# Five-group input chunks taken two at a time in front of a step, with longer rings for their results, in a Fourier-filter and MLP kernel

## The chip, the cores and the metric

The kernel runs on one core of a Trainium2 chip. Five engines work side by side, each through its own instructions in order: TensorE (PE in the profile, its weight loads PEld), VectorE (DVE), ScalarE (ACT), GpSimd (POOL) and SyncE (SP), which mostly issues DMAs. [...] The metric is the device time of one execution in microseconds, as the median of several runs. A difference of about 0.2% is what a measurement of this kernel can tell from none.

## The reference

The input `x` has 8 sequences of 3008 rows and 256 columns. A global filter in the frequency domain comes first, then an MLP with a hard swish:

```python
X = np.fft.rfft(x, axis=1)
Y = X * (filt_r + 1j * filt_i)[None, :, :]
y = np.fft.irfft(Y, n=x.shape[1], axis=1)      # (8, 3008, 256)
h = y.reshape(24064, 256) @ w_in               # 256 -> 2048
g = h * np.clip(h + 3.0, 0.0, 6.0) / 6.0
out = g @ w_out                                # 2048 -> 256
```

All of it is float32.

## The kernel before

**Two kinds of work, one stream.** The MLP is most of the work of TensorE. The 24064 rows are taken in 47 blocks of 512 rows (`NBLK`), held as 256 pairs of rows: for each pair two combined inputs, called c = 0 and c = 1. In a block, the 2048 hidden columns are taken in 8 parts of 256 (`NP`), so that there are 376 steps, counted by i = 8 k + p. A step's main loop body (the loop over `items` at the end) issues seven up products for block k, part p (`up_1` to `up_5`) and seven down products for the step before (`down`, numbered 1 to 7); it is a form of Strassen's scheme, so the up products need five sums of the inputs (tile `xt`, fields F1 to F5) beside the inputs themselves (tile `xn`).

Between the products the other engines work: up products collect in the PSUM banks `al` and `be`. ScalarE copies out of them (L990, L991 in `up_1`, L1002 in `up_2`, L1021 in `up_5`), VectorE adds (L1007, L1012), ScalarE applies the relu (L1026, twice a step), VectorE multiplies (L1031) and forms the sums of `g` that the down products need. Bank `al` is used four times a step and must have been read each time before the next product goes into it.

**The filter, spread over the steps.** The transform of the next sequences and its inverse are cut into small units. They are queued in a dictionary `plan` under a step and a place in the step's body, 0 to 4, and `do(place)` issues what stands there. Place 0 comes after `up_1`, place 1 after the first relu and ahead of `up_5`, place 2 at the end of the body. Places 3 and 4 are for units that take the banks `al` and `be`, or two banks of `psF` beside them (`a8_unit`, `b8_unit`, `bi8_unit`): place 3 comes ahead of the step, before the last step's down products, place 4 a little later, for what VectorE does with the unit's results. A step with something in place 3 has another order of its down products; in the step after it, `up_1` takes the product into `be` first and the one into `al` second.

**The last stage.** The inverse transform ends by giving the inputs of the MLP. Its work is cut into `chunks`: a sequence's 32 groups of 47 pairs each in chunks of five groups (235 pairs, "fives", `n_five`), and a rest of two or one groups (`n_unit`). `t4_load` brings a chunk's rows from DRAM with SP's queue into one of two halves of the tile `t4`. `n_five` issues 40 matmuls, each of 48 rows by 64 columns of weights and 47 columns of data (80 in the trace, as each float32 matmul is two there), into two banks of `psF`, and `ring` has ScalarE copy the results into `xn`, a ring of three blocks of pairs for each of the two halves of columns and each of c = 0 and 1 (L872; in two pieces where the ring turns round). The loop over `chunks` after `N_AT` and `FIVE_AT` decides at which step a chunk runs: in most blocks one five, in place 0 of step 1 or 6.

**The input sums.** When a chunk has completed block k, `ready` queues what forms the five sums in `xt`. Either `t_sums` does it with seven operations on GpSimd, or four copies by ScalarE (`t_copy`, L953: one of 512 columns, three of 256) and four DMAs by GpSimd's queue that add in place (`t_add`, L958, on the queue "POOLq"). With a chunk in step 1 the copies stand at the second and third step of the block and the last two adds at the sixth or seventh. `kinds` names six blocks for each sequence from the third on: "c", "a", "x" and three times "F"; `a8_unit` runs in c, a and x blocks, `b8_unit` at place 3 of step 2 and `bi8_unit` at place 3 of step 7 of each F block. All other blocks count as "t".

A remark on names: a helper records most matmuls of the last stage's rest and all MLP products under one line (L972, `strips`); the tiles tell them apart: `po<-w_all,g` are down products, `al<-xt,w_all`, `be<-xt,w_all` and those with `xn` are up products. `al<-xn,w_all` is the product of `up_5`, once a step.

## Time and profile before

| | |
|---|---|
| median of 3 runs | 2539.05 us (2538.61 to 2540.07) |
| the profiled execution | 2538.37 us, of which the span is 2536.3 us |
| granted TensorE clock | 1.000 |
| TensorE busy | 2521.5 us, 99% of the span |
| VectorE, ScalarE, GpSimd busy | 79%, 54%, 17% |
| matmuls of the fives (L899) | 3680 records, 63.6 us |
| copies into the rings (L872) | 162 from `psn`, 53.7 us |
| `t_copy` (L953) | 120, 51.9 us |

"Busy" for TensorE is a sum in which matmuls may overlap in the pipeline; where time passes is better read from the starts of successive instructions in the timeline. A line of the timeline has the start and the length in us, the engine, the line of the program, the operation, the tile written and the tiles read, the form, and how many equal instructions the line stands for; at its end, in brackets, an idle time before it and what ended that.

### The profile page before, as it was taken

To read this page: it belongs to the slowest core of one execution; us is meant where nothing else is said; L and a number is where in the kernel's file an instruction comes from. 1 tells how busy PE (TensorE), PEld (TensorE's weight loads), DVE (VectorE), ACT (ScalarE), POOL (GpSimd) and SP (SyncE) were. 2 spreads that over 40 slices of the span, in tenths; PEclk is the share of its full clock that TensorE was granted. 3 is DMA by queue.
4 is the path that set the end of the run, shared out by engine and by line. 5 is a ranking of instruction groups with operands and counts; after the bars stand their busy time and mean duration, and the time that the engine had idled before them with its cause. 6 is when DMAs were issued, how large, how long until landed. Compare 5 with 4: busy or idle time off the path is not lost.

```text
span 2536.3 us, 87284 instructions
## 1 busy us (share of the span) xinstructions
PE 2521.5 (99%) x37890; PEld 2007.7 (79%) x37890; DVE 2012.5 (79%) x3645; ACT 1363.8 (54%) x2836; POOL 423.6 (17%) x558
## 2 busy tenths in 40 slices
PE   8999999999999999999999999999999999999999
PEld 4478788888888788887888878887888878888887
DVE  6978888888787887878878788787887878767666
ACT  4554455555555555555555555555555555555554
POOL 3252111111211112111121110211102111111110
PEclk9999999999999999999999999999999999999999
DMA  8845556554445344444453443534424333211000
GB/s 237 237 121 166 162 136 157 160 135 100 119 98 137 98 103 121 97 128 101 110 125 90 125 111 95 135 88 117 122 66 96 88 103 92 54 40 27 19 22 26
DMA packets 210821, 276.91 MB, mean 109 GB/s; under 512 B 23274, under 2 KB 176392, under 8 KB 210054
## 3 DMA queue, kind: packets, MB, share of 16 engines
q1 hardware_dynamic: 163997, 200.76, 27.1%
q0 software_dynamic: 46112, 70.28, 14.2%
q8 instruction: 297, 4.87, 0.8%
q14 instruction: 86, 0.70, 0.1%
q10 hardware_dynamic: 329, 0.30, 0.0%
HBM read 164.38 MB, written 128.81 MB: 116 GB/s over the span
## 4 chain that ended last, share of the span: by engine, by line
PE 98%; DMA 1%; DVE 0%; SPq 0%; ACT 0%; issue 0%; POOL 0%; DVEq 0%
PE po L972 46%; PE al L972 26%; PE be L972 19%; PE psn L899 2%; PE be L608 1%; PE al L779 1%; PE psf L706 1%; DMA bits<-in_moe_w_in_dram 0%; PE psf L693 0%; DMA w_all<-in_x_dram 0%; PE psf L589 0%; DMA g_tmp<-t 0%; PE psn L972 0%; PE psf L763 0%; DMA wi<-wi_t 0%; DMA t<-g_tmp 0%
## 5 line engine op out<-in xcount | busy, mean ns | idle before, releaser
L972 PEld LDWEIGHTS po<-w_all,g 128*64 128x64 f32 x20808 | 1231.1, 137 | 262.5 <-issue 35.4
L972 PE MATMUL po<-w_all,g 128*64 128x128 f32 (+1 forms) x20808 | 1406.8, 274 | 0.0
L1026 ACT ACTIVATE r<-h,half_c 128x512 f32<-128x512 f32 x736 | 531.2, 722 | 335.5 <-DVE h L1007 323.4
L972 PE MATMUL al<-xt,w_all 128*64 128x256 f32 x4416 | 663.9, 379 | 0.1
L1031 DVE SCALAR_TENSOR_TENSOR g<-r,h 128x512 f32<-128x512 f32 x736 | 519.1, 705 | 147.0 <-ACT r L1026 133.5
L972 PE MATMUL be<-xt,w_all 128*64 128x256 f32 x2944 | 442.5, 379 | 0.0
L1007 DVE TENSOR_TENSOR h<-be,s 128x512 f32<-128x512 f32 x368 | 253.6, 689 | 170.3 <-PE be L972 138.5
L972 PEld LDWEIGHTS al<-xt,w_all 128*64 128x64 f32 x4416 | 285.0, 137 | 28.9 <-POOL w_all L469 1.0
L972 PEld LDWEIGHTS be<-xt,w_all 128*64 128x64 f32 x2944 | 209.0, 137 | 97.5
L1021 ACT ACTIVATE h<-al 128x256 f32<-128x256 f32 x368 | 141.4, 384 | 266.1 <-PE al L972 265.0
L1039 DVE TENSOR_TENSOR g<-g 128x512 f32<-128x512 f32 x367 | 255.7, 697 | 12.6
L1012 DVE TENSOR_TENSOR h<-al,s 128x256 f32<-128x256 f32 x368 | 155.7, 423 | 137.5 <-PE al L972 137.0
L972 PE MATMUL al<-xn,w_all 128*64 128x256 f32 (+1 forms) x1536 | 236.6, 388 | 1.0 <-DVE g L1031 0.6
L972 PE MATMUL be<-xn,w_all 128*64 128x256 f32 (+1 forms) x1536 | 236.4, 388 | 0.0
L991 ACT ACTIVATE s<-be 128x256 f32<-128x256 f32 x368 | 141.4, 384 | 148.8 <-PE be L972 145.8
L1002 ACT ACTIVATE s<-al 128x256 f32<-128x256 f32 x368 | 141.6, 385 | 123.9 <-PE al L972 120.8
L990 ACT ACTIVATE s<-al 128x256 f32<-128x256 f32 x368 | 141.7, 385 | 82.2 <-PE al L972 82.1
L1038 DVE TENSOR_TENSOR g<-g 128x256 f32<-128x256 f32 x367 | 161.9, 441 | 12.6
L1044 DVE TENSOR_TENSOR g<-g 128x256 f32<-128x256 f32 x367 | 155.5, 424 | 2.3
L972 PEld LDWEIGHTS be<-xn,w_all 128*64 128x64 f32 x1536 | 107.9, 137 | 53.4 <-issue 7.4
L958 POOL DMA_DIRECT2D xt<-xn x60 | 76.1, 1268 | 443.1 <-ACT xt L953 321.6
L1135 POOL TENSOR_TENSOR o<-p,o 128x256 f32<-128x256 f32 x45 | 33.1, 736 | 510.4 <-DVE o L1133 352.0
(199 smaller groups left out, 1976.9 us busy)
## 6 DMA issues: line engine op xcount, KB each, us to landing
g_tmp<-t POOLq DMA_DIRECT2D x96, 256.0 KB, 4.3
x_tmp<-in_x_dram SPq DMA_DIRECT2D x54, 384.0 KB
t<-g_tmp SPq DMA_DIRECT2D x168, 120.0 KB
ft<-f_tmp SPq DMA_DIRECT2D x36, 512.0 KB
t<-zp_tmp SPq DMA_DIRECT2D x36, 512.0 KB
o_tmp<-o SPq DMA_DIRECT2D x46, 256.0 KB
xt<-xn POOLq DMA_DIRECT2D x30, 384.0 KB, 6.7
zp_tmp<-y POOLq DMA_DIRECT2D x96, 96.0 KB, 3.6
```

Of the source, the lines that this page charges most:

```text
L972: nc.tensor.matmul(ps[ds(o, STRIP)], w[:, ds(o, STRIP)], x, skip_group_check=True, **kw)
L990: nc.scalar.activation(out=s[:, 0, :], in_=al, func=AXT.Copy)
L991: nc.scalar.activation(out=s5, in_=be[:, 1, :], func=AXT.Copy)
L1002: nc.scalar.activation(out=s[:, 1, :], in_=al, func=AXT.Copy)
L1007: nc.vector.tensor_tensor(out=st["h"][0].rearrange("p (a n) -> p a n", a=2), in0=be, in1=s, op=ALU.add)
L1012: nc.vector.tensor_tensor(out=st["h"][1][:, 256:512], in0=al, in1=s5, op=ALU.add)
L1021: nc.scalar.activation(out=st["h"][1][:, 0:256], in_=al, func=AXT.Copy)
L1026: nc.scalar.activation(out=r, in_=st["h"][i], func=AXT.Relu, bias=half_c, scale=1.0 / 6.0)
L1031: nc.vector.scalar_tensor_tensor(out=st["g", k, p][:, o:o + 2, :].rearrange("p a n -> p (a n)"), in0=st["r", i], scalar=1.0, in1=st["h"][i ...
L1038: v.tensor_tensor(out=g[:, G1, :], in0=g[:, G3, :], in1=g[:, G22, :], op=ALU.add)
L1039: v.tensor_tensor(out=g[:, G3:G2 + 1:2, :], in0=g[:, G3:G1 + 1, :], in1=g[:, G11:G11 + 1, :].broadcast_to([P, 2, 256]), op=ALU.subtract)
L1044: nc.vector.tensor_tensor(out=g[:, G4, :], in0=g[:, G12, :], in1=g[:, G2, :], op=ALU.subtract)
```

## The change

Five things change.

1. `xn` gets two lengths of ring: three blocks for c = 0 as before, four for c = 1. Since pieces turn round at different places now, `ring` issues one copy for each c where it issued one for both; for a five there was already one for each c. The table `wi`, used early on only, moves into the end of the ring's space.
2. A new unit, `n_ten`, issues two fives in a row: the first into two banks of `psF`, the second into `al` and `be`, then the four copies into the rings. It runs in place 3 of a step. The new loop puts such pairs at step 6 of "c" blocks and at step 3 of "x", some "F" and some "t" blocks; the first chunks of the kernel and one of the last fives keep their single form.
3. The units of two groups or one (`n_unit`) of the first seven sequences run at place 0 of step 1 of a block and use banks of `psF`; the form that used spare halves of `al` and `po` is gone. `t4_load` is queued earlier for the second of a pair.
4. `in_sums` takes the place of the queueing in `ready`. For a pair outside "c" and "t" blocks the first completed block gets its four copies in the pair's own step (two in place 1, two in place 2), two adds one step later and the other two three steps later. A second completed block is queued from the next block's step 1 on, as a single chunk there was.
5. Of the four `f_unit` after a `b8_unit`, the first two stand in place 4; before, only the first did, and the second was in place 2.

```diff
-RING = 3 * PAIRS
+RINGS = 3 * PAIRS, 4 * PAIRS
...
-    xn = const.tile([P, 2, 2, RING], FP32, name="xn")
+    xn = const.tile([P, 2, sum(RINGS)], FP32, name="xn")
+    xn_flat = xn.rearrange("p d n -> p (d n)")
+    wi = xn_flat[:, ds(2 * sum(RINGS) - 3 * NC, 3 * NC)].rearrange("p (a n) -> p a n", a=3)
...
+    def ring(i, a, m_, to, d, src):
+        for c in range(2):
+            done = 0
+            while done < m_:
+                r = (chunks[i][0] * HC * NA + to + done) % RINGS[c]
+                m = min(m_ - done, RINGS[c] - r)
+                nc.scalar.activation(out=xn[:, d, ds(c * RINGS[0] + r, m)], in_=src[c][..., ds(a + done, m)], func=AXT.Copy)
+                done += m
+
+    def in_sums(k, step, direct_=False):
+        if kinds.get(k - 1, "c") == "c" and not (step % NP == 1 and k - 1 in kinds):
+            return t_sums(k) if direct_ else at(step, t_sums, k)
+        if step % NP == 1:
+            b = 4 + (kinds[k - 1] == "x")
+            when = (1, 1), (2, 0), (2, 1), (2, 1), (2, 2), (2, 2), (b, 1), (b, 1)
+        else:
+            when = (0, 1), (0, 1), (0, 2), (0, 2), (1, 1), (1, 1), (3, 1), (3, 1)
+        for j, (s, place_) in enumerate(when):
+            plan.setdefault((step + s, place_), []).append((t_copy if j < 4 else t_add, (k, j % 4)))
+
+    def ready(i, fives=1):
+        t = pair(i)[0]
+        n = sum(pair(i + q)[1] for q in range(fives))
+        done = [k for k in range(t // PAIRS, (t + n) // PAIRS) if k]
+        for q, k in enumerate(done):
+            in_sums(k, n_at[i] if q == 0 else (k - 1) * NP + (1 if k - 1 in kinds else 2), q == 0)
...
+    def n_ten(i):
+        out_ = five(i, [psF.tile([P, 512], FP32, name="psn", tag="f") for c in range(2)])
+        more = five(i + 1, [psU.tile([P, 512], FP32, name=x) for x in ("al", "be")])
+        out_()
+        more()
+        ready(i, 2)
...
-        N_AT = {"c": ((6, 6), (6, 6), (6, 6)), "F": ((1, 1), (1, 1), (6, 6)), "t": ((2, 4), (2, 4), (6, 6))}
-        FIVE_AT = {"c": (6, 3, 6), "a": (1, 1, 5), "x": (1, 1, 5), "F": (1, 0, 1), "t": (4, 2, 4)}
+        N_FIRST = {2: (3, 4), 3: (10, 10), 4: (11, 11), 5: (17, 17), 6: (25, 25)}
+        TEN_AT = {"c": 6, "x": 3, "F": 3, "t": 3}
...
+            if i in N_FIRST:
+                s0, s1 = N_FIRST[i]
+            elif b == 0:
+                s0 = s1 = (k - 1) * NP + 1
+            elif i - 1 in tens:
+                s0 = s1 = n_at[i - 1]
+            elif five_ and i + 1 < len(chunks) and len(chunks[i + 1][1]) == NJ:
+                tens[i] = s0 = s1 = (k - 1) * NP + TEN_AT[kinds.get(k - 1, "t")]
+            elif b < B - 1:
+                s0 = s1 = (k - 1 if ends else n_at[i - 1] // NP + 1) * NP + 1
+            else:
+                s0, s1 = ((k - 1) * NP + s for s in ((4, 4) if five_ else (2, 4)))
...
             at(max(stored, n_at[i - 2] + 1), t4_load, i)
-            if five:
+            if i in tens:
+                plan.setdefault((s1, 3), []).append((n_ten, (i,)))
+            elif i - 1 in tens:
+                continue
+            elif five_:
                 at(s1, n_five, i)
...
-                    plan.setdefault((f_at[i], 4), []).append((f_unit, (n, i)))
-                if n == 1 or i % 4:
+                if n > 1 and i % 4 < 2:
+                    plan.setdefault((f_at[i - i % 4], 4), []).append((f_unit, (n, i)))
+                else:
                     at(f_at[i], f_unit, n, i)
```

More of the change, by code (lines that the diff above doesn't have):

```diff
@@ L295 @@
     edges = edge.rearrange("p (j n) -> p j n", n=TOK)
-    wi = const.tile([P, 3, NC], FP32, name="wi")
     wi2 = const.tile([P, 2, HC], FP32, name="wi2")
@@ L301 @@
     t4 = const.tile([P, 2 * NJ, D], FP32, name="t4")
-    xn = const.tile([P, 2, 2, RING], FP32, name="xn")
+    xn = const.tile([P, 2, sum(RINGS)], FP32, name="xn")
+    xn_flat = xn.rearrange("p d n -> p (d n)")
+    xn0 = [xn[:, d, 0:2 * RINGS[0]].rearrange("p (c n) -> p c n", c=2) for d in range(2)]
+    wi = xn_flat[:, ds(2 * sum(RINGS) - 3 * NC, 3 * NC)].rearrange("p (a n) -> p a n", a=3)
     w_all = const.tile([P, NP, 2, 7, P], FP32, name="w_all")
@@ L538, in zt @@
     def zt(dh):
-        return (xn.rearrange("p a c n -> p (a c n)"), xs.rearrange("p i j d -> p (i j d)"))[dh]
+        return (xn_flat[:, 0:4 * RINGS[0]], xs.rearrange("p i j d -> p (i j d)"))[dh]
     def copy(dve, to, ps):
@@ L865, in t4_load @@
                     q += m
-    def ring(i, a, m_, to, out, src):
-        done = 0
-        while done < m_:
-            r = (chunks[i][0] * HC * NA + to + done) % RING
-            m = min(m_ - done, RING - r)
-            nc.scalar.activation(out=out(ds(r, m)), in_=src[:, :, ds(a + done, m)], func=AXT.Copy)
-            done += m
-    def ready(i):
-        t, n = pair(i)
-        k = t // PAIRS
-        if (t + n) // PAIRS > k > 0:
-            if n_at[i] % NP == 1 and k - 1 in kinds:
-                st["xt", k] = xtp.tile([P, 5, PAIRS], FP32, name="xt")
-                b = 4 + (kinds[k - 1] == "x")
-                for j, (step, place_) in enumerate(((1, 1), (2, 0), (2, 1), (2, 1), (2, 2), (2, 2), (b, 1), (b, 1))):
-                    plan.setdefault((n_at[i] + step, place_), []).append((t_copy if j < 4 else t_add, (k, j % 4)))
-            else:
-                t_sums(k)
@@ L888, in n_five @@
-    def n_five(i, ends_step=False):
+    def ring(i, a, m_, to, d, src):
[16 more added lines that the diff above has]
+            plan.setdefault((step + s, place_), []).append((t_copy if j < 4 else t_add, (k, j % 4)))
@@ L889, in n_five, with five @@
+    def ready(i, fives=1):
[4 more added lines that the diff above has]
+            in_sums(k, n_at[i] if q == 0 else (k - 1) * NP + (1 if k - 1 in kinds else 2), q == 0)
+    def five(i, banks):
         b, js, o, n = chunks[i]
         s0 = i % 2 * NJ
-        banks = [psU.tile([P, 512], FP32, name=x) for x in ("al", "be")] if ends_step else [
-            psF.tile([P, 512], FP32, name="psn", tag="f") for c in range(2)]
@@ L900, in n_five @@
                                          groups[r, j, :], start=True, stop=True)
-        for c in range(2):
-            ring(i, 0, n, o, lambda at_: xn[:, :, c, at_], ps[c])
+        return lambda: ring(i, 0, n, o, slice(0, 2), ps)
+    def n_five(i):
+        five(i, [psF.tile([P, 512], FP32, name="psn", tag="f") for c in range(2)])()
         ready(i)
+    def n_ten(i):
[4 more added lines that the diff above has]
+        ready(i, 2)
     def n_unit(i, dh):
-        if spare[i]:
-            ps = st["po", n_at[i] // NP][2][:, 1, :, :].rearrange("p u m -> p (u m)") if dh else st["al"][:, 256:512]
-        else:
-            ps = psF.tile([P, 512], FP32, name="psn", tag="f")
+        ps = psF.tile([P, 512], FP32, name="psn", tag="f")
         b, js, o, n = chunks[i]
@@ L912, in n_unit @@
             w = edges[0:2 * ATOM, FIRST.index(j), :] if i >= TAIL and j else ones[0:2 * ATOM, j, :]
-            strips(ps[:, ts(q, TOK)], t4[0:2 * ATOM, i % 2 * NJ + q, ts(dh, P)], w, start=not spare[i], stop=True)
+            strips(ps[:, ts(q, TOK)], t4[0:2 * ATOM, i % 2 * NJ + q, ts(dh, P)], w, start=True, stop=True)
         for q, a, m, to in TO.get(i, [(q, 0, NA, o + q * NA) for q in range(len(js))]):
-            ring(i, a, m, to, lambda at_: xn[:, dh, :, at_], ps[:, ts(q, TOK)].rearrange("p (c n) -> p c n", c=2))
+            p_ = ps[:, ts(q, TOK)].rearrange("p (c n) -> p c n", c=2)
+            ring(i, a, m, to, dh, [p_[:, c, :] for c in range(2)])
         if dh:
@@ L935, in n_first @@
                 strips(ps[:, ts(q, TOK)], t4[:, j - 1, ts(dh, P)], edges[:, FIRST.index(j), :], start=False, stop=True)
-            to = xn[:, dh, :, 0:PAIRS]
+            to = xn0[dh][:, :, 0:PAIRS]
             if c == 0:
@@ L941, in n_first @@
             nc.scalar.activation(out=to[:, :, NJ * NA:], in_=ps[:, 0:2 * NX].rearrange("p (h a) -> p h a", h=2), func=AXT.Copy)
-            nc.scalar.activation(out=xn[:, dh, :, ds(PAIRS, NA - NX)],
+            nc.scalar.activation(out=xn0[dh][:, :, ds(PAIRS, NA - NX)],
                                  in_=ps[:, 2 * NX:TOK].rearrange("p (c a) -> p c a", c=2), func=AXT.Copy)
     def xb(k, d, c):
-        return xn[:, d, c, ts(k % 3, PAIRS)]
+        return xn[:, d, ds(c * RINGS[0] + k % (3 + c) * PAIRS, PAIRS)]
     F1, F3, F5, F2, F4 = range(5)
     def t_copy(k, j):
+        if j == 0:
+            st["xt", k] = xtp.tile([P, 5, PAIRS], FP32, name="xt")
         t, (s0, s1) = st["xt", k], (xb(k, d, 1) for d in range(2))
@@ L1089, in plain_up @@
             for d in range(2):
-                strips(st["h"][i], w_in[p][:, 2 * d + i, :], xn[:, d, :, 0:PAIRS], start=d == 0, stop=d == 1)
+                strips(st["h"][i], w_in[p][:, 2 * d + i, :], xn0[d][:, :, 0:PAIRS], start=d == 0, stop=d == 1)
             relu(i)
@@ L1328 @@
         at(2, x_load, 1, 2)
-        n_at, spare = {0: -2, 1: -2}, {}
+        n_at, tens = {0: -2, 1: -2}, {}
         kinds = {}
@@ L1334 @@
                 kinds[first[n] - 7 + d] = kind
-        N_AT = {"c": ((6, 6), (6, 6), (6, 6)), "F": ((1, 1), (1, 1), (6, 6)), "t": ((2, 4), (2, 4), (6, 6))}
-        FIVE_AT = {"c": (6, 3, 6), "a": (1, 1, 5), "x": (1, 1, 5), "F": (1, 0, 1), "t": (4, 2, 4)}
-        N_FIRST = {0: ((3, 4),), 1: ((), (2, 2), (3, 3)), 2: ((1, 1),), 3: ((1, 1),)}
-        in_block = {}
-        for i in range(2, len(chunks)):
-            in_block.setdefault(pair(i)[0] // PAIRS, []).append(i)
+        N_FIRST = {2: (3, 4), 3: (10, 10), 4: (11, 11), 5: (17, 17), 6: (25, 25)}
@@ L1342 @@
+        TEN_AT = {"c": 6, "x": 3, "F": 3, "t": 3}
         stored = 0
         for i in range(2, len(chunks)):
-            k = pair(i)[0] // PAIRS
-            head = chunks[i][2] == 0
-            same = in_block[k]
-            at_, kind = same.index(i) + 1 if len(same) > 1 else 0, kinds.get(k - 1, "t")
-            steps = N_FIRST[k - 1][at_] if k - 1 in N_FIRST else (FIVE_AT[kind][at_],) * 2 if len(chunks[i][1]) == NJ else N_AT[kind][at_]
-            if head and len(same) == 1:
-                steps = (6, 6)
@@ L1351 @@
-            s0, s1 = ((k - 1) * NP + s for s in steps)
-            five = len(chunks[i][1]) == NJ
+            b, js, o, n = chunks[i]
+            k, five_ = pair(i)[0] // PAIRS, len(js) == NJ
+            ends = (pair(i)[0] + n) // PAIRS > k
+            if i in N_FIRST:
[10 more added lines that the diff above has]
+                s0, s1 = ((k - 1) * NP + s for s in ((4, 4) if five_ else (2, 4)))
@@ L1353 @@
             n_at[i] = s1
-            spare[i] = kind == "c" and at_ == 1
-            if head:
+            if o == 0:
                 stored = s0 - 3 + (k == first[1])
             at(max(stored, n_at[i - 2] + 1), t4_load, i)
-            if five:
+            if i in tens:
[3 more added lines that the diff above has]
+            elif five_:
                 at(s1, n_five, i)
-                continue
-            at(s0, n_unit, i, 0)
@@ L1362 @@
-            at(s1, n_unit, i, 1)
+            else:
+                at(s0, n_unit, i, 0)
+                at(s1, n_unit, i, 1)
         A_AT = (3, 10, 18, 21)
@@ L1448 @@
                     plan.setdefault((f_at[i], 3), []).append((b8_unit, (n, i // 4)))
-                    plan.setdefault((f_at[i], 4), []).append((f_unit, (n, i)))
-                if n == 1 or i % 4:
+                if n > 1 and i % 4 < 2:
+                    plan.setdefault((f_at[i - i % 4], 4), []).append((f_unit, (n, i)))
+                else:
                     at(f_at[i], f_unit, n, i)
```

## The prediction

> **What bounds the kernel now.** I read the engine shares and the chain of waits first, then the groups by shape, then the timeline around one input chunk of five groups ("a five"). The page says that TensorE is the bound and that almost nothing holds it up:

> ```profile
> PE 2521.5 (99%) x37890; PEld 2007.7 (79%) x37890; DVE 2012.5 (79%) x3645; ACT 1363.8 (54%) x2836; POOL 423.6 (17%) x558
> ...
> PE 98%; DMA 1%; DVE 0%; SPq 0%; ACT 0%; issue 0%; POOL 0%; DVEq 0%
> ```

> So only two things can move the time: what TensorE spends, and new waits of TensorE. Next, a five at the beginning of a step and what surrounds it (timeline, us from the start):

> ```profile
> 717.02 0.60 PE L972 MATMUL al<-xn,w_all 128*64 128x256 f32 x4
> ...
> 718.75 0.60 PE L972 MATMUL be<-xn,w_all 128*64 128x256 f32 x4
> ...
> 719.19 0.60 PE L972 MATMUL be<-xt,w_all 128*64 128x256 f32 x4
> ...
> 719.72 1.38 PE L899 MATMUL psn<-wai,t 48*64 48x47 f32 x80
> ...
> 721.03 0.66 PE L972 MATMUL po<-w_all,g 128*64 128x128 f32 x8
> 721.15 1.02 ACT L872 ACTIVATE xn<-psn 128x470 f32<-128x470 f32 x2 [0.93 <-PE psn L899]
> ...
> 721.52 0.60 PE L972 MATMUL al<-xt,w_all 128*64 128x256 f32 x4
> ...
> 724.56 0.60 PE L972 MATMUL al<-xn,w_all 128*64 128x256 f32 x4
> ```

> The up product of `up_5` (al<-xn) marks each step: 724.56 - 717.02 = 7.54 us here against 6.08 us in a step with nothing extra, so a five costs 1.46 us. Its parts: the five starts 0.53 after the product before it, where products follow each other at 0.43 (entry 0.10); it lasts 1.31 to the next product; that product takes 0.49 instead of 0.44 (0.05). Within the 1.38 us its matmuls go out in 20 rows of four; the last starts 0.23 before the end, so 1.15 us hold 19 intervals and a first one that is 0.02 longer: 0.0585 us for a row, 1.17 for 20. What is left, 1.46 - 1.17 = 0.29 us, is paid for changing from one shape of matmul to another and back.

> Third, ScalarE and TensorE around the border of a step with a unit (a group of 32-row matmuls in `do(3)`), since the change puts new ScalarE work there:

> ```profile
> 731.78 0.72 ACT L1026 ACTIVATE r<-h,half_c 128x512 f32<-128x512 f32 x1 [1.28 <-DVE h L1007]
> ...
> 732.29 0.60 PE L972 MATMUL al<-xn,w_all 128*64 128x256 f32 x4
> 732.41 0.61 ACT L953 ACTIVATE xt<-xn 128x512 f32<-128x512 f32 x1
> ...
> 732.94 0.38 ACT L1021 ACTIVATE h<-al 128x256 f32<-128x256 f32 x1
> ...
> 733.36 0.72 ACT L1026 ACTIVATE r<-h,half_c 128x512 f32<-128x512 f32 x1
> ...
> 733.59 0.60 PE L972 MATMUL al<-xt,w_all 128*64 128x256 f32 x4
> ...
> 734.24 0.38 ACT L990 ACTIVATE s<-al 128x256 f32<-128x256 f32 x1 [0.16 <-PE al L972]
> ...
> 734.89 0.60 PE L972 MATMUL al<-xt,w_all 128*64 128x256 f32 x4
> ...
> 790.01 0.71 ACT L953 ACTIVATE xt<-xn 128x256 f32<-128x256 f32 x2
> ```

> Three products in a row use bank al, and ScalarE reads it between them (L1021, then L990). ScalarE is only 54% busy, but here its order decides when al is free: L1021 ends at 733.32, 0.27 before the next al product, and L990 at 734.62, 0.27 before the one after. The last line shows two copies of 256 columns, 0.40 each, in 0.71: they stand 0.31 apart, so neighbours overlap by 0.09.

> **The change, part by part.** The sum is made against the profiled execution, 2538.37 us (span 2536.3 and 2.07 around it), 0.68 under the median 2539.05; I apply the difference to the median.

> *Fives in pairs.* Working out the schedule from the loops gives 20 pairs: six in "c" steps (place 6), twelve at place 3 of an "x" or "F" block, two in the last blocks. Each replaces two fives at 1.46 by one run: 1.46 + 1.17 = 2.63 instead of 2.92, so -0.29 (-0.294 from unrounded starts), 20 x 0.294 = -5.9 us. No row shows two fives in succession. From below: no gain, since the second cannot beat the cadence of 0.0585. From above: one more entry of 0.10 each, +2.0 in all. I take 0, as the shape stays. Running them ahead of the step (the order of steps with units) costs nothing by itself: a unit step and the one after take 7.73 + 5.65 = 13.38, 1.22 above two plain ones, and the unit accounts for 1.22 (1.07 from 725.96 to 727.03, and again 0.10 and 0.05).

> *Banks al and be.* The second five needs al read by L1021 (ended 1.03 us after the al<-xn product starts; the second five starts over 2 us after it) and must give al back before `up_1`. From the pair's start: the first two ring copies at 1.43 and 1.89 (721.15 - 719.72, and 1.02 for two), al's at 2.60, be's at 3.06, al free at 3.16 + 0.05 (the shortest distance in the trace from such a read to the next product). `up_1` wants al at 2.48 + 1.15 = 3.63: margin 0.41, cost nothing. Bounds 0 to 0.53 a pair (rival two).

> *Input sums at other steps.* In twelve pairs (x and F) `in_sums` now queues the four `t_copy` in the pair's own step: two in place 1, ahead of L1021, two in place 2, ahead of the next step's L990. Before, only one stood ahead of an L1021 here, the others after L991 or after a relu with room. From the relu at 731.78 as zero: copy of 512 at 0.63, copy of 256 at 0.63 + 0.52 = 1.15 (0.61 less the overlap 0.09), L1021 at 1.46 (now 1.16), relu 0.42 later at 1.88, copies at 2.51 and 2.82, L990 at 3.13, ended 3.51, al free 3.56. The third al product stood at 734.89 - 731.78 = 3.11. It waits 0.45, of which 0.08 already at the second. Nothing later gives TensorE this back. Twelve times 0.45 = +5.4 us. Bounds: 0 if L1021 and L990 find ScalarE free all the same, 1.02 if copies don't overlap (below). I take 0.45, which every spacing shown in the rows supports. The "c" pairs have only two short copies there (al free at 1.68 against 1.81): nothing. The last two use POOL sums: nothing.

> If each ScalarE operation held the engine for its whole recorded time (relu 0.72, copies 0.61 and 0.41, L1021 0.38, relu 0.72, copies 0.41 twice, L990 0.38, and 0.08 of hand-over), al would be free at 4.13, the wait would be 1.02, and twelve of them 12.2; the kernel would end near 2545. The two copies at 790.01, 0.40 each in 0.71, speak against it, so the sum goes by the overlap. [...]

> *Adds by POOL DMA.* In those steps the first add starts some 6 us later, after the copies. In the x block shown here it was issued at 735.91, and the last landed 19.5 us later, 10.2 before its use by the be product at 765.64; all chains last 12.5 to 24 us. The pair also delays the use by about 2-3 us, which leaves some 6 us: nothing, unless the chain passes 26. On POOL's queue `z8_store` stands behind them as before, and waits for DVE anyway.

> *Loads.* A pair's two `t4_load` start together, three steps (18 us) ahead in "c", more elsewhere; before, some had two steps. On SP's queue the `half_load` behind them moves by four to ten issues of about 0.5-0.8 us and is wanted ten steps later: nothing; without this room TensorE would wait for the rows.

> *Ends and small pieces.* The units of [1, 0] move to place 1 and cost 0.65 in both positions. Each ring copy is split in two, about +0.05 a piece; L1002 stands behind them at 1820.88 and hardly moves. In the last batch L1002 shifts by 0.4 with over 0.6 of room. The lone [0] unit waited 0.22 for L990 at 334; away from there it saves, with 0.05 of another step, -0.3. The second `f_unit` goes ahead of h on DVE: 1.2 us into an idle stretch of 1.60 before h at 783.59. Longer rings and the moved wi table issue nothing.

> Sum: -5.9 - 0.3 + 5.4 = -0.8 us: 2538.2 us.

> **Rivals.** *One: the copies are hidden.* If L1021 and L990 keep their places, the gain stands alone: 2539.05 - 6.2 = 2532.9. For it: ScalarE is idle 46%. Against it: the room at both places is 0.27 - 0.05 us and the copies add 0.3 and 0.6.

> *Two, on the other side: emptying the banks.* If the first five's ring copies go only after the second five's matmuls, al's copy is third in the queue: 2.60 + 0.92 + 0.56 + 0.05 = 4.13 against 3.63, then be 0.03: 0.53 x 20 = +10.6, 2548.8. It decides from 0.41 us of delay on. Against it: L990 starts 0.65 after its own product though two more products were issued ahead of it, so ScalarE waits for its own data. [...]

> *Three: sums too late.* Were the chain of adds to need 27 us or more, each of twelve blocks would wait a microsecond or so: 2550. Against it: the longest seen is 24.

> [...]

> **How the numbers follow.** Forecast (gain nearly cancelled by ScalarE) 0.62; one 0.20; two 0.10; three 0.04; four 0.04. 0.2% of the time, 5.1 us, is about what a measurement here can tell: under 2534.0 is faster, above 2544.1 slower. The forecast is inside (own range 2537.5 to 2541, from the second five's entry and 0.40 to 0.50 per wait), only rival one is faster, two to four are slower: 0.20, 0.62, 0.18. The range must reach rival one, and leave out two to four: 2532.4 to 2543.5.

> **What would show it.** In the changed profile: runs of 160 matmuls at L899's successor with about 2.48 us to the next product; no wait of TensorE inside them; at x and F pairs the third al product some 0.45 late behind L990, listed as a wait for ScalarE; step pairs of c without it. Wrong if those waits are absent (then near 2533), if al or be waits for ring copies, if xt waits for DMA, or if the second five restarts slowly.

## The result, and the profile after

The changed kernel takes 2552.06 us (median of 6 runs, 2549.50 to 2554.36) against 2539.56 us (median of 6, 2537.35 to 2541.20): a ratio of 1.005, with a 95% interval from 1.0039 to 1.0061. The forecast was 2538.2 with a range of 2532.4 to 2543.5, so the change is slower where no difference was forecast, and the time lies above the range. The profiled execution took 2551.41 us, its span is 2549.3 us.

The page of the changed kernel, answering the two lines shown of before (busy times, the chain that ended last). The line between them, the instruction transfers, stands in the page of before in the same words:

```profile
PE 2525.1 (99%) x37890; PEld 2026.6 (79%) x37890; DVE 2005.5 (79%) x3645; ACT 1366.5 (54%) x2890; POOL 418.4 (16%) x558
...
q8 instruction: 297, 4.87, 0.8%
...
PE 94%; ACT 2%; DVE 2%; issue 1%; DMA 1%; SPq 0%; DVEq 0%; POOL 0%; ACTq 0%
```

TensorE issues the same 37890 matmuls and is still the bound, but the chain now spends 2% on ScalarE, 2% on VectorE and 1% on "issue", where before it spent none. The waits of TensorE by line (total, times, longest, us) say where:

```profile
PE be L905 <- issue: 2.8, 3, 1.9
PE po L987 <- issue: 2.6, 3, 1.2
PE po L987 <- DVE o L1149: 2.1, 7, 0.3
PE al L905 <- issue: 1.7, 3, 0.7
```

L905 is the matmul of a five, L987 a strip of a product, L1149 the add of `out_4`. "Issue" is idle time that no semaphore explains. The list is only a pointer: it counts a gap from the modelled end of a matmul, and it leaves ScalarE out, whose waits end at the weight loads (below).

The two traces can be compared step by step, since the up product al<-xn marks each step in both. From the first mark to the last the kernel before takes 2394.86 us and the changed one 2409.43: +14.57. (The first mark came 1.65 us earlier in the changed one, but in the profiled kernels that do the same work ahead of that mark it came anywhere between 129.2 and 134.0 us, so 1.65 can't be put down to the change.) The 14.57 are, from the lengths of the steps:

| where | steps | us |
|---|---|---|
| 20 pairs instead of 40 single fives, -0.294 each | all blocks | -5.9 |
| step behind an x or F pair, 6.09 instead of 5.64 (three of them up to 6.25) | 12 | +5.9 |
| x1 steps, 6.61 instead of 6.08 (step 41: 6.68), and 0.05 in each next one | 7 | +4.1 |
| pairs in which, or right behind which, TensorE stops for "issue": 3.55 at step 38 (1.5 of it a lower clock, below), 0.3 to 1.4 at nine others | 10 | +10.4 |
| the rest: small pieces saved, single steps grew by up to 0.34 | | +0.1 |

These make 14.6. The first two rows were in the forecast, the third and fourth were not.

A pair without a stop looks as foreseen. The changed kernel's timeline around an x pair, TensorE and ScalarE:

```profile
735.73 1.38 PE L905 MATMUL psn<-wai,t 48*64 48x47 f32 x80
...
737.16 1.02 ACT L875 ACTIVATE xn<-psn 128x470 f32<-128x470 f32 x2 [0.61 <-PE psn L905]
...
738.22 1.31 PE L987 MATMUL po<-w_all,g 128*64 128x128 f32 x20
...
738.33 0.63 ACT L875 ACTIVATE xn<-al 128x254 f32<-128x254 f32 x2
738.84 0.57 ACT L875 ACTIVATE xn<-be 128x470 f32<-128x470 f32 x1
...
739.36 0.60 PE L987 MATMUL al<-xt,w_all 128*64 128x256 f32 x4
```

From the pair's start to the next product there are 738.22 - 735.73 = 2.49 us, forecast 2.48; al is read empty at 738.96, 0.40 ahead of its next product, which is 0.35 of room once the 0.05 of the forecast are taken off, forecast 0.41; the step is 8.716 long, 2.64 above a plain one.

A pair with a stop is the c pair of step 86:

```profile
650.15 1.38 PE L905 MATMUL psn<-wai,t 48*64 48x47 f32 x80
...
651.95 0.27 PE L905 MATMUL al<-wai,t 48*64 48x47 f32 x2
...
652.83 0.25 PE L905 MATMUL al<-wai,t 48*64 48x47 f32 x1 [0.60 <-issue]
...
653.54 0.66 PE L987 MATMUL po<-w_all,g 128*64 128x128 f32 x8
```

In the middle of the second five, with no semaphore wait shown, the starts of matmuls pause from 651.99 to 652.83. The DMA of the same stretch (649.9 to 651.6 us) holds one single packet, and it is no data:

```profile
DMA packets 1, 0.02 MB, mean 10 GB/s; under 512 B 0, under 2 KB 0, under 8 KB 0
...
q8 instruction: 1, 0.02, 4.5%
```

It starts at 650.20 in the trace, 2.63 us before the matmuls go on. The 297 packets of this queue carry 16384 bytes each. Over TensorE's 76145 records (weight loads, matmuls, semaphores and drains) that is 63.9 bytes for each, so a packet is, as an estimate from these counts, a piece of 256 instructions of 64 bytes: 297 x 256 is 76032. The suspicion is that a pair, 320 instructions in 2.3 us, outruns them. Between the first mark and the end of the steps, 256 instructions never took less than 4.2 us before; in the changed kernel they take as little as 1.85.

The longest stop, at step 38, has a second part. Rows of the windows view, for this stop and for the pair without one; the number behind the last bracket is TensorE's granted clock:

```profile
334.50:337.00 2.50, 2.06 (x43) 1.97 (x44) 0.00 (x0) 0.90 (x2) 2.34 (x4) 0.56 0.51 135
...
735.50:738.30 2.80, 2.80 (x168) 2.58 (x166) 1.85 (x4) 2.04 (x4) 0.00 (x0) 1.00 0.36 106
```

No matmul starts from 332.85 to 334.94, and from 334.82 on the records grant a clock of 0.5 for 3.41 us. The 20 strips behind the pair take 2.18 us to the next product instead of 1.14. Of the 3.55 us, about 2.05 are the pause and 1.5 the low clock behind it.

The step behind an x or F pair, weight loads of TensorE and the work of ScalarE, answering the lines of before around 731.78:

```profile
743.59 0.93 ACT L968 ACTIVATE xt<-xn 128x512 f32<-128x512 f32 x2
744.42 0.36 ACT L1036 ACTIVATE h<-al 128x256 f32<-128x256 f32 x1
744.82 0.73 ACT L1041 ACTIVATE r<-h,half_c 128x512 f32<-128x512 f32 x1
745.45 0.70 ACT L968 ACTIVATE xt<-xn 128x256 f32<-128x256 f32 x2
746.06 0.36 ACT L1005 ACTIVATE s<-al 128x256 f32<-128x256 f32 x1
...
744.84 0.20 PEld L987 LDWEIGHTS al<-xt,w_all 128*64 128x64 f32 x4 [0.35 <-ACT h L1036]
...
746.47 0.20 PEld L987 LDWEIGHTS al<-xt,w_all 128*64 128x64 f32 x4 [0.36 <-ACT s L1005]
```

Two copies stand ahead of L1036 and two ahead of L1005; each of the next two al products waits for ScalarE, 0.07 and 0.38 us as seen in the product starts, 0.45 in all. Neighbouring copies overlap, 0.93 us for one of 512 and one of 256 columns, as the forecast took it.

And an x1 step, whose five has gone (VectorE, then TensorE):

```profile
722.32 1.22 DVE L524 TENSOR_TENSOR xs<-xs,wa 128x1024 f32<-128x1024 f32 x1
723.45 0.68 DVE L1046 SCALAR_TENSOR_TENSOR g<-r,h 128x512 f32<-128x512 f32 x1
...
725.58 0.41 DVE L1149 TENSOR_TENSOR o<-po,o 128x256 f32<-128x256 f32 x1
...
726.04 1.09 PE L987 MATMUL po<-w_all,g 128*64 128x128 f32 x16 [0.30 <-DVE o L1149]
```

The down product at 726.04 should follow the al product of 725.14 by 0.43 and follows by 0.90. It waits for `out_4` to read its bank, and `out_4` stands in VectorE's queue behind `half_sums` (L524, 1.22 us). Before, a five of 1.46 us on TensorE gave VectorE the time for it: behind the same `half_sums` (L522 there), `out_4` (L1134) ended 1.05 us ahead of the product.

```profile
718.97 1.22 DVE L522 TENSOR_TENSOR xs<-xs,wa 128x1024 f32<-128x1024 f32 x1
...
722.22 0.41 DVE L1134 TENSOR_TENSOR o<-po,o 128x256 f32<-128x256 f32 x1
...
723.68 1.04 PE L972 MATMUL po<-w_all,g 128*64 128x128 f32 x16
```

### The profile page after: what moved, and what is told of

The parts are those of the page before. It is cut to its first block, busy times and chain, and to the rows that moved or that the text cites. A ratio compares the mean times of both kernels' runs of the same rounds, so it can differ in the third digit from the quotient of the medians.

```text
span 2549.3 us, 87331 instructions
## 1 busy us (share of the span) xinstructions
PE 2525.1 (99%) x37890; PEld 2026.6 (79%) x37890; DVE 2005.5 (79%) x3645; ACT 1366.5 (54%) x2890; POOL 418.4 (16%) x558
## 3 DMA queue, kind: packets, MB, share of 16 engines
q8 instruction: 297, 4.87, 0.8%
## 4 chain that ended last, share of the span: by engine, by line
PE 94%; ACT 2%; DVE 2%; issue 1%; DMA 1%; SPq 0%; DVEq 0%; POOL 0%; ACTq 0%
PE po L987 44%; PE al L987 25%; PE be L987 18%; PE psn L905 1%; PE be L610 1%; PE al L781 1%; PE al L905 1%; ACT xt L968 1%; PE psf L708 1%; ACT r L1041 1%; PE psf L695 0%; PE psf L591 0%; DVE h L1022 0%; PE psn L987 0%; DMA g_tmp<-t 0%
## 5 line engine op out<-in xcount | busy, mean ns | idle before, releaser
L987 PEld LDWEIGHTS po<-w_all,g 128*64 128x64 f32 x20808 | 1246.5, 137 | 259.9 <-issue 39.2
L987 PE MATMUL po<-w_all,g 128*64 128x128 f32 (+1 forms) x20808 | 1416.9, 275 | 3.9 <-DVE o L1149 2.1
L987 PE MATMUL al<-xt,w_all 128*64 128x256 f32 x4416 | 671.7, 380 | 1.6
L1046 DVE SCALAR_TENSOR_TENSOR g<-r,h 128x512 f32<-128x512 f32 x736 | 513.4, 698 | 174.0 <-ACT r L1041 158.3
L987 PE MATMUL be<-xt,w_all 128*64 128x256 f32 x2944 | 447.3, 379 | 0.3 <-issue 0.3
L987 PEld LDWEIGHTS al<-xt,w_all 128*64 128x64 f32 x4416 | 291.1, 137 | 42.1 <-ACT s L1005 4.3
L987 PEld LDWEIGHTS be<-xt,w_all 128*64 128x64 f32 x2944 | 213.7, 137 | 90.8 <-issue 0.6
L1036 ACT ACTIVATE h<-al 128x256 f32<-128x256 f32 x368 | 141.2, 384 | 249.1 <-PE al L987 248.0
L987 PE MATMUL al<-xn,w_all 128*64 128x256 f32 (+1 forms) x1536 | 239.5, 389 | 1.0 <-DVE g L1046 0.6
L987 PE MATMUL be<-xn,w_all 128*64 128x256 f32 (+1 forms) x1536 | 238.7, 388 | 0.0
L1005 ACT ACTIVATE s<-al 128x256 f32<-128x256 f32 x368 | 141.6, 385 | 88.7 <-PE al L987 87.9
L987 PEld LDWEIGHTS be<-xn,w_all 128*64 128x64 f32 x1536 | 111.2, 137 | 50.0 <-issue 7.4
```

Source lines behind the costliest of these rows:

```text
L987: nc.tensor.matmul(ps[ds(o, STRIP)], w[:, ds(o, STRIP)], x, skip_group_check=True, **kw)
L1005: nc.scalar.activation(out=s[:, 0, :], in_=al, func=AXT.Copy)
L1036: nc.scalar.activation(out=st["h"][1][:, 0:256], in_=al, func=AXT.Copy)
L1046: nc.vector.scalar_tensor_tensor(out=st["g", k, p][:, o:o + 2, :].rearrange("p a n -> p (a n)"), in0=st["r", i], scalar=1.0, in1=st["h"][i ...
```

## The experiments

The rule that I took for the instruction supply before these runs, a fit to the changed kernel's trace: there TensorE stops at an instruction whose number in its stream is the same modulo 256 each time (the first late matmul record is number 193 or 194), when the last 320 instructions up to it took less than about 5 us. Why 320 and not 256: in that trace, at the places of this number where the matmuls pause for 0.5 us or more, the last 320 took up to 5.12 us, and only two places without a stop lie below that (4.79 and 5.01); the last 256 took up to 4.66 there, and ten places without a stop lie below. The trace also shows one transfer for every 256 instructions, which starts, at the median, 250 instructions ahead of the next of these places: about one piece ahead, an estimate from these counts. Nothing here shows more than one fetched in advance.

**Shifting the instruction stream, first try.** In the changed kernel (and, as a control, in the one before):

```diff
-        keep_warm(1)
+        for i in range(64):
+            nc.tensor.matmul(ps[0:STRIP, 0:8], zero[:, P:P + STRIP], zero[:, 0:8], start=True, stop=True)
         direct(NU - 2)
```

> The changed kernel with 64 tiny matmuls (64 columns of weights, 8 columns of data) in place of one warming matmul at 48 us, well before the first pair; nothing else differs. Each is one weight load and one matmul, so every later TensorE instruction moves on by 128 in its stream. Theory 1 (TensorE runs out of instructions): its instructions are fetched in transfers of 16384 bytes, 256 instructions each; in the changed kernel TensorE stops at the first instruction of such a piece, always at the same remainder modulo 256 of the instruction count, when the 320 instructions ending there took less than about 5 us. By that rule, worked out from the matmul starts of the changed kernel, a shift of 128 puts 19 of 20 pairs on a bad place, 1 to 2.4 us each, 31 us in all where unshifted it gives 6 (11 were seen): the time rises by about 25 us, to 2577 (2565 to 2590), and the stops move: in the F pairs, which had none, about 2 us each just after the pair. Theory 2 (the stops come from what lies around the pairs: the banks al and be, the late loads, the transfers): the stops stay where they were, c pairs 0.5 to 1 us and F pairs none, and the time is 2552 plus at most 3.3 for the tiny matmuls themselves.

> The same 64 tiny matmuls in the kernel before. Theory 1: single fives put 160 instructions into 1.2 us and leave over 5 us for each 320, by the rule no place of the 256 stalls, so nothing but the cost of the tiny matmuls in the prologue (0 to 3.3 us): 2538 to 2543, and no step after the prologue differs from before by more than 0.1 us. Theory 2 says the same. If steps do get longer here, the rule of 5 us is wrong.

Measured, in one execution each: 2563.4 us for the changed kernel and 2548.34 for the one before, beside 2538.1. Both expectations were built on a wrong count: such a matmul over 128 rows is two weight loads and two matmuls, so the stream moved by 252 instructions, 4 short of a whole piece. And the 64 tiny matmuls took 10.9 and 10.3 us, where at most 3.3 was put down: one took 0.117 us until the granted clock fell to 0.5 in their midst, at 51.8 and 51.7 us, and 0.213 after it. The clock stayed there for 13.7 and 10.2 us, and the first mark came 13 and 9 us later. From the first mark on the changed kernel took 2408.4 us, against 2409.4 unshifted. This is no test of the 25 us that were foreseen. It is a small one of the rule, though: relative to the pair every stop inside a pair of the changed kernel came exactly 4 instructions later (in c pairs 252 to 256 at step 38, 248 to 252 at 86, 242 to 246, 236 to 240, 230 to 234), while the work around the pairs was the same. The kernel before grew by 1.2 us after its first mark, in four single steps, up to 0.47 in one where none was to change by more than 0.1. None of the four shows a stop for "issue", and no step with a five changed.

**Spreading the copies.**

```diff
-            when = (0, 1), (0, 1), (0, 2), (0, 2), (1, 1), (1, 1), (3, 1), (3, 1)
+            when = (0, 1), (1, 0), (1, 1), (1, 1), (1, 2), (1, 2), (3, 1), (3, 1)
```

> The changed kernel with the four t_copy of x and F pairs at places (0,1), (1,0), (1,1), (1,1) of the pair's step and the next instead of (0,1), (0,1), (0,2), (0,2), and the first two adds at (1,2): the spacing that the kernel before had, one at a time ahead of L1036 (h<-al). If the 0.45 us in the step after each x and F pair is ScalarE's queue, those twelve steps go from 6.09 back to 5.64 and the time falls by 5.4, to 2546.7 (2544 to 2549). If it is something else after a pair (banks al and be, or instructions), they stay at 6.09 and the time at 2552.

Measured: 2546.99 us (6 runs, 2545.84 to 2550.59) where before is at 2538.10, a ratio of 1.0037 (1.0024 to 1.0051). ScalarE's timeline at the same place:

```profile
743.55 0.61 ACT L968 ACTIVATE xt<-xn 128x512 f32<-128x512 f32 x1
744.18 0.38 ACT L1036 ACTIVATE h<-al 128x256 f32<-128x256 f32 x1
744.60 0.72 ACT L1041 ACTIVATE r<-h,half_c 128x512 f32<-128x512 f32 x1
745.48 0.38 ACT L1005 ACTIVATE s<-al 128x256 f32<-128x256 f32 x1 [0.16 <-PE al L987]
```

With one copy ahead, L1036 and L1005 follow their products again; L1005 waits for TensorE and not the other way round. All twelve steps went from 6.09 (three from up to 6.25) to 5.64 or 5.70, 5.4 us together. ScalarE's queue was nearly the whole of that row.

**Moving the sums of VectorE.**

```diff
-        SUM_AT = ((-10, -2), (2, 7), (13, 14), (15, 16))
+        SUM_AT = ((-10, -2), (2, 7), (13, 14), (15, 18))
...
-        SUM2_AT = ((1, 3), (4, 5), (10, 12), (15, 16))
+        SUM2_AT = ((1, 3), (4, 5), (10, 12), (15, 18))
```

> The changed kernel with the half_sums of the last quarter two steps later (last entry of SUM_AT and SUM2_AT 18 instead of 16), where the pair of the x block gives VectorE 2.6 us more. If the x1 steps are longer by 0.53 us because these sums stand in VectorE's queue ahead of out_4 (L1149) and the five that covered them has gone, the six x1 steps go from 6.61 to 6.08, each next step loses 0.05, and the time falls by about 3.5, to 2548.5. If out_4 is late for another reason, the x1 steps stay at 6.6.

Measured: 2548.10 us (7 runs, 2546.47 to 2550.36), a ratio of 1.0039 (1.0027 to 1.0051). The x1 step on VectorE and TensorE:

```profile
722.98 0.41 DVE L1149 TENSOR_TENSOR o<-po,o 128x256 f32<-128x256 f32 x1
...
724.12 1.04 PE L987 MATMUL po<-w_all,g 128*64 128x128 f32 x16
724.99 0.60 PE L987 MATMUL al<-xn,w_all 128*64 128x256 f32 x4
```

`out_4` now ends 0.73 us ahead of the product that needs the bank. The six x1 steps fell from 6.61 to 6.08 (-3.2 us) and the next ones by 0.05. Step 41, where another VectorE job stands, kept its 0.6.

**Shifting the instruction stream by half a piece.**

```diff
             if j in (4, 12):
                 keep_warm(1)
+            if j == 20:
+                for i in range(32):
+                    nc.tensor.matmul(ps[0:STRIP, 0:8], zero[:, P:P + STRIP], zero[:, 0:8], start=True, stop=True)
```

> The changed kernel with 32 tiny matmuls ahead of the last two of the first eight units of the prologue, where TensorE sat idle. The first shift missed: a tiny matmul over 128 rows is recorded as two weight loads and two matmuls, so 64 of them in place of one were 252 instructions, 4 short of a whole piece of 256, and every stop moved by only 4. Here 32 of them are 128 instructions. Theory 1 (instructions come in pieces of 256; TensorE stops at the first instruction of a piece when the 320 ending there took less than about 5 us): 19 of 20 pairs fall on a bad place; the c pairs stop after the pair, the x and F pairs too, 1 to 2.4 us each. The rule gives 31 us in all where it gives 6 for the changed kernel (11 were seen): 2577 (2565 to 2592), with the prologue at most 3 us longer. F pairs, which never stopped, tell most: steps of 8.7 become 10 or more in that step and the next. Theory 2 (the stops come from banks, loads or transfers around the pairs): c pairs stop as before, F pairs do not, 2552 plus at most 3.

Measured, in one execution: 2576.73 us. From first mark to last it took 2429.7, 20.3 more than the changed kernel; the rest lies ahead of the first mark, where the clock was 0.5 for 6.8 us. The pair of step 99, which had run through (735.73 above), and the waits of this run:

```profile
742.05 1.38 PE L905 MATMUL psn<-wai,t 48*64 48x47 f32 x80
...
744.89 0.20 PE L905 MATMUL be<-wai,t 48*64 48x47 f32 x1 [0.43 <-issue]
...
745.26 0.98 PE L987 MATMUL po<-w_all,g 128*64 128x128 f32 x14
```

```profile
PE al L905 <- issue: 7.3, 4, 3.1
PE be L905 <- issue: 6.2, 4, 2.7
```

The order of all other work is the same, and the stops changed places: four of the six c pairs, among them the one that had lost 3.55, now run through, and the other two lose 0.5 and 0.7; all six x pairs stop inside, none of which had, and all F pairs inside or just behind. Over four kernels (the changed one, both shifts, the spread copies) 27 pairs have such a pause of over 0.4 us between two matmuls of a five, and in all of them the first late matmul has number 193 or 194 modulo 256, and starts 2.16 to 2.69 us after the start of the last instruction transfer. That settles the cause of the stops. The rule's sizes held less well: the total came out (31 us of stops forecast, 10.4 + 20.3 = 30.7 measured), but by luck, since its parts did not. F pairs lost 0.5 to 0.9 instead of about 2, except the one at step 299, c pairs at most 0.7 instead of 1 to 2.4, and four pairs (51, 147, 243, 299) lost 4.4 to 5.8. Their pauses were 2.7 to 3.4 us long, because the transfer itself began only 2.3 to 3.2 us after the pair did. The other 1.7 to 2.8 us of each, 8.7 together, are a cost that the rule did not have: the granted clock fell to 0.5 at each of the four, for 3.4 or 6.8 us, as at step 38 of the changed kernel. That leaves at most 22 us for the stops.

Over all eleven traces the clock falls between the first mark and the last seven times. Each time it falls during, or within 1 us after, a pause inside a pair of more than 2 us, and there are seven of these; the 29 shorter pauses inside pairs, up to 1.81 us, left it at 1.0. At step 38 the two can be told apart: with the copies spread or the sums moved the pause was 1.8 us, the clock stayed at 1.0, and the step lost 1.7 to 1.8 instead of 3.55.

As to the late transfers: in the stretch from 1057.5 to 1061.5 us the hardware queue that brings `t4` moved 882 packets, in a stretch with a short stop (741.5 to 745.5) 609. The trace of before bears this out: from TensorE's 150th instruction of a piece to the start of the next transfer the median is 1.26 us where the DMA engines are under 20% busy in the 3 us that follow, and 2.72 where they are over 80% busy. That is a correlation; no run changes the loads alone.

**The two fives of a pair apart in one step.** `n_ten` does the first five only; the second goes to place 0 of the same step, behind `up_1`, in two psF banks:

```diff
-        out_ = five(i, [psF.tile([P, 512], FP32, name="psn", tag="f") for c in range(2)])
-        more = five(i + 1, [psU.tile([P, 512], FP32, name=x) for x in ("al", "be")])
-        out_()
-        more()
+        five(i, [psF.tile([P, 512], FP32, name="psn", tag="f") for c in range(2)])()
+
+    def n_second(i):
+        five(i + 1, [psF.tile([P, 512], FP32, name="psn", tag="f") for c in range(2)])()
         ready(i, 2)
...
+                plan.setdefault((s1, 0), []).append((n_second, (i,)))
```

> The changed kernel with the two fives of each pair in the same step, but the second one after up_1's products instead of right behind the first, in the usual two banks, and emptied by itself. Theory 1: some 110 other instructions and 3.5 us lie between the two, so 320 instructions take over 5 us nearly everywhere: the stops (about 11 us) go, and each pair pays once more for the change of shape, 20 times 0.29 = 5.9: about 2547 (2544.5 to 2549.5); the x1 steps (+0.53) and the steps behind x and F pairs (up to +0.45) stay. If the stops came from the late loads or from what else was moved, they stay and the time is 2558.

Measured: 2551.28 us (2549.43 and 2553.14), a ratio of 1.0049 (1.0031 to 1.0067): 4 us above what was expected. The profiled execution explains half. From mark to mark it took 2406.29, 3.14 less than the changed kernel. The stops inside and behind pairs are gone but for some 0.4 at step 331; but a second five there costs 0.45 (c and F: 9.604 for 9.152, 9.167 for 8.716) or 0.51 (x), not 0.29. The rest of the 4 us lies ahead of the first mark, which came at 133.98 in this execution, with the clock at 0.5 for 6.8 us on the way; the other execution took 2549.43, inside the expected range. So splitting ends the stops, and costs about as much as it saves.

**A mixture, with and without a shift of 40.** Pairs in c and F blocks only, the fives of x and of the last batch at two steps, copies spread; the first with 10 tiny matmuls in the place of the 32 above, the second without:

```diff
+            elif i in apart:
+                s0 = s1 = apart[i]
...
-                tens[i] = s0 = s1 = (k - 1) * NP + TEN_AT[kinds.get(k - 1, "t")]
+                kind = kinds.get(k - 1, "t")
+                if kind in "cF":
+                    tens[i] = s0 = s1 = (k - 1) * NP + TEN_AT[kind]
+                else:
+                    s0 = s1 = (k - 1) * NP + {"x": 1, "t": 3}[kind]
+                    apart[i + 1] = s1 + (2 if kind == "x" else 1)
```

> A mixture: pairs only in c and F blocks (12 of them); the fives of x blocks apart again, at steps 1 and 3 (the first gives VectorE its cover at x1 back), those of the last batch at steps 3 and 4; the copies spread; and 10 tiny matmuls in the prologue, 40 instructions, which by theory 1 put the c pairs where they do not stop and leave the F pairs where they do not. Theory 1: against before 12 x 0.294 = 3.5 us saved, 0.6 lost in the one step 41, no stop above 0.3 us in any c pair: 2535.2 (2533 to 2537.5) where before is at 2538.1. Theory 2: the c pairs stop as in the changed kernel, 0.5 to 1 us each and 1.8 in the first, and it comes out as the next run does.

> The same mixture without the 10 tiny matmuls. Theory 1: the six c pairs stand where they stood in the changed kernel and five or six of them stop, 0.5 to 1 us each and 1.8 in the first, some 5.5 us in all: 2540.7 (2538.5 to 2543). Theory 2: no difference from the run with the tiny matmuls beyond 1.5 us.

Measured: 2537.65 us with the shift (11 runs), a ratio to before (2538.67) of 0.9995 (0.9987 to 1.0004), and 2544.16 without (8 runs), 1.0025 (1.0015 to 1.0036). The 40 instructions are worth 6.5 us, 5.5 were expected. The c pair of step 86 with the shift:

```profile
646.66 1.38 PE L906 MATMUL psn<-wai,t 48*64 48x47 f32 x80
...
649.15 1.31 PE L988 MATMUL po<-w_all,g 128*64 128x128 f32 x20
```

2.49 us again, and five of the six c pairs are free of stops; the one of step 38 still pauses for 0.42 and loses 0.5. Without the shift step 38 lost 3.7, of which the low clock is 1.7, and three others 0.5 to 0.8. The mixture still came out 2.4 above the expected 2535.2, or 1.9 counted from before, and just above its range: step 299 stopped for 1.7 (this pair lies elsewhere in its piece than the other F pairs), and step 54 grew by 1.1, where VectorE waits for a transfer (y<-zp_tmp).

The kernel without the shift also shows that a single five can be hit. At step 147, where one five stands alone, TensorE paused between two down products for 1.75 us, at the same place of a piece and 2.83 us after the start of a transfer, and the step lost 1.7; step 99 lost 0.4 in the same way.

**Fewer pairs.** The same, with ten pairs (c blocks from step 86 on, F blocks 67, 115, 163, 211, 259) and every other five at its step of before:

```diff
-                if kind in "cF":
+                if b > 1 and kind in "cF" and i != 47 or i == 12:
...
-                    s0 = s1 = (k - 1) * NP + {"x": 1, "t": 3}[kind]
-                    apart[i + 1] = s1 + (2 if kind == "x" else 1)
+                    s0 = s1 = (k - 1) * NP + {8: 6, 47: 1, 50: 6, 52: 4}.get(i, 1)
+                    apart[i + 1] = s1 + {8: 3, 45: 7, 50: 4}.get(i, 8)
```

> The mixture with fewer pairs: only ten are left (the c and F blocks of the second to fifth batches, the c block of the sixth and the first F pair, at step 67); every other five stands alone at the step that it had in the kernel before, so that step 41 and step 54 get their cover back and the pair at step 299, which stopped for 1.7 us in the mixture, is gone. Copies spread, and the same 10 tiny matmuls. Theory 1: no pair stops, 10 x 0.294 = 2.9 us and 0.3 from the small unit saved, about 0.6 lost in single steps as the mixture showed them (215, 275 and the steps behind F pairs): 2.6 us below before, 2536.1 (2535 to 2537.5) where before is at 2538.7, which is as much as five rounds can just tell. If some pair stops after all, 2538 or more.

Measured: 2535.57 us (11 runs, 2533.57 to 2537.54) against 2537.95, a ratio of 0.9990 (0.9981 to 0.9999): clearly faster than the changed kernel, and below the one before by the 0.1% that was expected, a difference that the interval only just tells from none. No pair stops. In the profiled execution, the slowest of the eleven, 2.2 are lost at step 54 and 0.7 at step 246, where VectorE's y<-t (L628) waits for the zp_tmp transfer.

## Why the prediction was wrong

- **What bounds the kernel: right.** TensorE's cost and its new waits are all that moved the time.
- **Fives in pairs, -0.294 each: right.** Every pair without a stop has it (8.716 against a forecast of 6.08 + 2.63).
- **The second five, "I take 0, as the shape stays": the step that failed, for 10.4 us.** Where TensorE doesn't stop, its entry is indeed 0 and its cadence unbroken. But the bound from above, one more entry of 0.10 each and 2.0 in all, looked at the array only. A row of 160 instructions in 1.2 us lived from what had been fetched wherever it stood in the kernel before; 320 in 2.3 us don't always. Of the 10.4 us, 1.5 are the low clock behind the longest pause, which the forecast did not price either. The line that would have told, 297 instruction packets, 4.87 MB, was on the page: a pair takes more than one piece in 2.3 us, and the pieces are on average 8.5 us apart (2536 us over 297). A bound from it (nowhere behind the first mark did TensorE use up 256 instructions in less than 4.2 us before) would have widened the range to the slow side.
- **Taking the fives away from x1: priced as pure gain, and wrong by 4.1 us.** The forecast charged each five 1.46 us and did not ask what VectorE did meanwhile. The run with the moved sums gave 3.5 of it back; step 41 kept its 0.6.
- **The copies, twelve times 0.45: right** in place, size and cause. The four copies took the room that the rows showed, and spreading them gave 5.4 back. The long reading of ScalarE's times, copies without overlap (the fourth rival, 1.02), did not happen: two copies of 512 and 256 take 0.93 instead of 1.02, as the row at 790.01 had it.
- **Banks al and be: right.** 0.35 us of room for a forecast 0.41; rival two did not happen.
- **Adds, loads, rings: right.** No product waits for xt from a transfer, and none of t4's loads is waited for inside a pair.
- **Ends and small pieces:** 0.3 put down; steps 18 and 19 saved 0.3, steps 33 and 34 lost 0.2, and with the single steps nothing is left of it.
- **The rivals:** none was the one that happened. The terms that were priced, -0.8 in the forecast, came to +0.1; the two that were missing made +14.5.

## What to carry over

Before TensorE work is packed more densely, count instructions as well as rows: here 256 of them passed in as little as 1.85 us, and where TensorE stopped it went on only 2.16 to 2.69 us after a transfer had started, without any semaphore to show it. Where it stopped depended on how many instructions lay ahead, so that ten harmless matmuls elsewhere were worth 6.5 us. Look at the granted clock behind a long stop, too: at seven stops here it added 1.5 to 2.8 us. A piece of work that is taken off the critical engine's path at some place was also time for the other engines there: look at what they had queued at that place before its whole length is booked as gain. And a gain of 0.3 us a piece is only worth having where the neighbours have room for it, as those of the ten pairs of the last run had.
